# Attention with two gated layers on one core: narrow reciprocals of the softmax sums, and a copy that repeats them

## The chip, the cores and the metric

One core of a Trainium2 chip runs the whole program in one launch. The metric is the time of one execution on the device in microseconds. The engines are PE (matmuls), DVE, ACT, POOL, and SP, which issues the DMAs; each works through its own queue of instructions in order and waits there on semaphores.

## The reference

Causal attention with a decay bias, then a layer with cos as its gate, then an RMS norm and a layer with SiLU as its gate. Four sequences of 576 tokens, 8 heads of 64, 512 columns, all in fp32:

```python
scores = scale * q @ k.T + minimum(-(cum_i - cum_j), 0)     # masked above the diagonal
attn = exp(scores - max) ; attn = attn / (sum(attn) + 1e-9)
x = attn @ v                        # 2304 tokens x 512
h = x @ w_in ; y = (h * cos(h)) @ w_out
xn = y / rms(y) * rms_g
out = (silu(xn @ w_gate) * (xn @ w_val)) @ w_out2
```

## The kernel before

Heads are worked on in 16 pairs (two heads side by side in the 128 partitions). Each pair has two parts: "a" with the first 256 queries and "b" with the other 320; part a is one unit of work, part b is two. For a unit PE forms the scores (lines 433 and 438, and 460 and 461 for the last 64 queries of both heads, called p), DVE copies them out of PSUM with their minimum as a by-product (tile mn, lines 445 and 464), ACT takes the exponentials and their sums (e, ep and rs, line 472), PE transposes the exponentials (line 504), a copy brings them to SBUF (tile P), and PE multiplies them by v (line 549).

The result of line 549 has queries along the free dimension, and must be multiplied by one over the sum of each query. The function norm, called once for a unit, prepares that: POOL scales the sums of two to four columns (line 480, tile rn), DVE takes the reciprocal (line 489) and writes each column 64 times side by side (tile rb, 128x128 for a unit of part b, 128x256 for part a), PE transposes rb in the function av (line 533), so that each query's factor stands in the 64 partitions of its head, a copy brings that to tile xu, and DVE multiplies line 549's result by it. The factors of the p rows go through line 531, which reads rn itself; so line 491 takes the reciprocal of that one column in place.

The two layers are gemms in split form: each fp32 value is a leading part and a residue in a shorter format, and three of the four products are added (lines 651 and 657). The weights are brought into that form in the function chunk: a shift of the exponent on ACT or POOL (line 365 or 364), bit work on POOL and DVE (368, 369, 371), then a copy and a subtraction (288 or 295, and 299 or 301) into tiles wi and ws. These conversions run beside attention, and those of the second layer beside the first layer. Activations (xa, g) are split in the same way.

The order of all instructions is set before the kernel runs by a planner in the same file (class Plan). Each operation names one or more engines with an entered cost, a due time, and the tiles it reads and writes; the planner steps through the engines by these costs and, for an operation with a choice (function copy: ACT, DVE or POOL; function two: DVE or POOL), takes the engine that would be done first. What comes out is one fixed queue for each engine. Line 489 is entered with 128 m + 80 ns, 208 or 336. Gemms have later due times than attention and are put where PE would wait.

Of the kernel before, what the change touches and what calls it, by code (L numbers as in the profile page):

```python
# [195 lines left out]
def dve2(n):  # L196
    return 0.52 * n + 68
# [10 lines left out]
def pool1(n):  # L208
    return 0.833 * n + 161
# [7 lines left out]
def attention_moe_moe(ctx, tc, q2, k2, vp, s, w_in, w_out, w_gate, w_val, w_out2, rms_g, out):  # L217
    nc = tc.nc
    pe, act, dve, pool, sp = nc.tensor, nc.scalar, nc.vector, nc.gpsimd, nc.sync
    plan = Plan()  # L220
# [61 lines left out]
    def on(e, ns, fn):  # L282
        return [(e, ns, fn)]

    def copy(o, i, n, r, w, scale=1.0, psum=False, engines=("ACT", "DVE", "POOL"), **kw):
        alts = []
        if "ACT" in engines:
            alts.append(("ACT", (act_p if psum else act_s)(n), lambda: act.activation(o(), i(), AF.Copy, scale=scale)))  # L288
        if "DVE" in engines:
            if scale == 1.0:  # L290
                alts.append(("DVE", (dve1 if psum else dve2)(n), lambda: dve.tensor_copy(o(), i())))
            else:
                alts.append(("DVE", dve2(n), lambda: dve.tensor_scalar(out=o(), in0=i(), scalar1=scale, scalar2=None, op0=ALU.mult)))
        if "POOL" in engines and not psum:
            alts.append(("POOL", pool1(n), lambda: pool.tensor_scalar(out=o(), in0=i(), scalar1=scale, scalar2=0.0, op0=ALU.mult, op1=ALU.add)))
        return plan.op(alts, r, w, **kw)
# [61 lines left out]
    def chunk(src, w, after=()):  # L358
        raw, g = raw_r.new(), cv_r.new()
        load(raw, lambda: src.bitcast(I32).rearrange("p (c t) -> p c t", t=2), 1 << 19, [], [raw], after=after)  # L360
        top, low = (lambda: raw()[:, :, 1]), (lambda: raw()[:, :, 0])
        v = lambda: g().bitcast(I32)
        plan.op([
            ("POOL", pool1(512), lambda: pool.tensor_scalar(out=g(), in0=top().bitcast(F32), scalar1=2.0 ** -112, scalar2=1.0, op0=ALU.mult, op1=ALU.mult)),
            ("ACT", act_s(512), lambda: act.activation(g(), top().bitcast(F32), AF.Copy, scale=2.0 ** -112)),  # L365
        ], [raw], [g])

        plan.op(on("POOL", pool1(512), lambda: pool.tensor_scalar(out=top().bitcast(F32), in0=top().bitcast(F32), scalar1=0.0, scalar2=1.0, op0=ALU.mult, op1=ALU.mult)), [], [raw])  # L368
        plan.op(on("DVE", dve1(512), lambda: dve.scalar_tensor_tensor(  # L369
            out=top(), in0=low(), scalar=29, in1=top(), op0=ALU.logical_shift_right, op1=ALU.bitwise_or)), [], [raw])  # L370
        plan.op(on("DVE", dve1(512), lambda: dve.scalar_tensor_tensor(  # L371
            out=v(), in0=v(), scalar=3, in1=top(), op0=ALU.logical_shift_left, op1=ALU.bitwise_or)), [raw], [g])
        copy(lambda: w()[:, 0, :], g, 512, [g], [w])
        two(lambda: w()[:, 1, :], g, lambda: w()[:, 0, :].bitcast(F32), 512, [g], [w])
        return w
# [30 lines left out]
    class Part:  # L406
# [69 lines left out]
        def norm(self, keys):  # L476

            rn, rs, a = self.rn, self.rs, self.col[keys[0]]
            b = a + len(keys)
            plan.op(on("POOL", 204, lambda: pool.tensor_scalar(  # L480
                out=rn()[:, a:b], in0=rs()[:, a:b], scalar1=1e-9, scalar2=float(2.0 * np.pi), op0=ALU.add, op1=ALU.mult)), [(rs, self.col[k]) for k in keys], [(rn, a)])
            rb, p = self.rb, "p" in keys
            if self.c == "a":
                o, i = (lambda: rb()), (lambda: rn()[:, :4].rearrange("p (e t) -> p t e", e=2))
            else:
                t = 0 if p else 1
                o, i = (lambda: rb()[:, t:t + 1]), (lambda: rn()[:, a:a + 2].unsqueeze(1))
            m = 1 if self.c == "b" else 2
            plan.op(on("DVE", 128 * m + 80, lambda: dve.reciprocal(out=o(), in_=i().unsqueeze(3).to_broadcast([128, m, 2, 64]))), [(rn, a)], [(rb, a)])  # L489
            if p:  # L490
                plan.op(on("DVE", 150, lambda: dve.reciprocal(out=rn()[:, 2:3], in_=rn()[:, 2:3])), [], [(rn, a)])

        def tr(self, e, i):
            tr = self.bank("T")
# [104 lines left out]
    for b in (s_b, cum):  # L599
# [4 lines left out]
        out=cum()[:, :S], data0=ones.to_broadcast([128, S]), data1=s_b()[:, :S], initial=0.0, op0=ALU.mult, op1=ALU.add)), [(s_b, 0)], [(cum, 0)])  # L604
# [6 lines left out]
    for i, (t, mid) in enumerate(((0, 63), (1, 191), (2, 319), ("p", 543), (3, 447))):  # L611
        o, w = DS[t]
# [9 lines left out]
            out=to(), in0=src(), scalar=halves[:, 1:2], in1=to().bitcast(F32), op0=ALU.mult, op1=ALU.add)), [raw], [(ds, o)], **kw)  # L622
# [126 lines left out]
    for k in range(8 * NB1):  # L749
        j, m = divmod(k, 8)  # L750
# [75 lines left out]
    for n, (d, f, w) in enumerate(names):  # L826
        plan.now = tick_at(8 * NB1)
        b = chunk(w[f], ws_r.new(), [ticks[W3_FROM + n * (W3_TO - W3_FROM) // len(names)]])
# [5 lines left out]
    for n, (d, f, w) in enumerate(names[:len(slots)]):  # L834
# [4 lines left out]
        b = w3[d, f] = slots[n][1].new(slots[n][2])  # L839
# [4 lines left out]
    for n in range(NB2 * F2):  # L844
# [25 lines left out]
        if f == F2 - 1:  # L870
            plan.now = unit_at(n)
            for t in range(3):
                o = u_r.new()
# [59 lines left out]
```

## Time and profile before

| | |
|---|---|
| three runs | 1106.91, 1107.06 and 5998.42 us, median 1107.06 |
| the profiled execution | 1107.06 us, its span 1105.3 us |
| instructions in the span | 17231 |
| DMA | 134.86 MB, 122 GB/s on average |

Times below are microseconds from the start of the span. The profile's page gives busy time by engine and the chain of work that ended last; the trace gives the same by stretch, by line and by tile. Matmuls are pipelined and their ends are modelled: a PE that is shown as busy need not be at its peak, and PEld is the weight load that overlaps it. Line 299 is the helper two on DVE, 301 the same on POOL; 288, 291 and 295 are the helper copy on ACT, DVE and POOL.

### The profile page before, as it was taken

How to read it: one execution, taken by the hardware profiler on the slowest of the kernel's cores; microseconds unless marked ns; L12 is line 12 of the kernel's file. 1: busy time of each engine (PE TensorE's matmuls, PEld its weight loads, DVE VectorE, ACT ScalarE, POOL GpSimd, SP SyncE). 2: the span in 40 equal slices, each digit the busy share in tenths (PEclk: the TensorE clock that was granted, in tenths of full speed). 3: DMA queues.
4: the chain of work that ended last, by engine and by line, in shares of the span. 5: the costliest groups of instructions: out<-in, count | busy, mean ns of one | idle time of the engine just before them, and what ended most of it. 6: DMA issues, size and time to landing. Idle time of an engine off the chain costs nothing.

```text
span 1105.3 us, 17231 instructions
## 1 busy us (share of the span) xinstructions
PE 1084.6 (98%) x6602; PEld 943.7 (85%) x6602; DVE 556.8 (50%) x1182; ACT 515.2 (47%) x1072; POOL 141.7 (13%) x213
## 2 busy tenths in 40 slices
PE   7989999999999999999999999999999999999998
PEld 5667776777788999988999999999999999999997
DVE  8888989675534677778677431121221211211211
ACT  5778889777743565656565332121211211211211
POOL 4631444111000012102010000000000000000000
PEclk9999999999999999999999999999999999999999
DMA  5763775534292364645564951010100100100000
GB/s 198 267 210 127 234 239 186 177 113 139 75 349 76 117 219 172 198 172 176 188 211 130 383 195 48 1 58 1 33 25 1 58 1 1 44 1 1 29 1 29
DMA packets 60595, 134.86 MB, mean 122 GB/s; under 512 B 8544, under 2 KB 28512, under 8 KB 60512
## 3 DMA queue, kind: packets, MB, share of 16 engines
q1 hardware_dynamic: 60512, 133.75, 35.7%
q8 instruction: 52, 0.85, 0.3%
q14 instruction: 31, 0.25, 0.1%
HBM read 94.40 MB, written 39.32 MB: 121 GB/s over the span
## 4 chain that ended last, share of the span: by engine, by line
PE 83%; DVE 9%; ACT 3%; issue 3%; POOL 1%; DMA 1%; DVEq 0%; POOLq 0%; ACTq 0%
PE bank L651 43%; PE bank L657 29%; PE bank L549 3%; PE bank L504 3%; PE bank L433 2%; DVE cv L371 2%; DVE e L445 1%; DVE rb L489 1%; DVE raw L369 1%; DVE u L299 1%; PE bank L741 1%; DVE ws L299 1%; PE bank L460 1%; ACT P L288 1%; ACT e L472 0%
## 5 line engine op out<-in xcount | busy, mean ns | idle before, releaser
L299 DVE TENSOR_TENSOR u<-bank,u 128x512 f32<-128x512 f32 (+1 forms) x144 | 89.8, 623 | 338.7 <-PE bank L651 269.2
L657 PE MATMUL bank<-wr,g 128*128 128x512 f32 x942 | 234.0, 396 | 0.6 <-ACT g L288 0.5
L651 PE MATMUL bank<-xa,wi 128*128 128x256 f32 x1728 | 220.8, 283 | 0.0
L651 PEld LDWEIGHTS bank<-xa,wi 128*128 128x128 f32 x1728 | 215.0, 188 | 6.0 <-issue 0.6
L288 ACT ACTIVATE g<-u 128x512 fp32r<-128x512 f32 (+1 forms) x132 | 76.1, 577 | 280.1 <-DVE u L299 280.0
L657 PEld LDWEIGHTS bank<-wr,g 128*128 128x128 f32 x942 | 173.1, 188 | 35.6 <-ACT g L288 1.2
L299 DVE TENSOR_TENSOR g<-u,g 128x384 fp32r<-128x384 f32 (+1 forms) x130 | 81.2, 625 | 63.4 <-ACT g L288 61.9
L651 PE MATMUL bank<-xb,wi 128*128 128x384 f32 x528 | 102.9, 339 | 0.0
L651 PE MATMUL bank<-xb,wr 128*128 128x384 f32 x528 | 101.0, 335 | 0.0
L651 PEld LDWEIGHTS bank<-xb,wi 128*128 128x128 f32 x528 | 93.3, 188 | 3.0 <-DVE xb L299 1.7
L651 PEld LDWEIGHTS bank<-xb,wr 128*128 128x128 f32 x528 | 93.1, 188 | 2.1
L767 ACT ACTIVATE u<-bank,quarter 128x512 int32<-128x512 f32 x72 | 49.2, 684 | 71.1 <-PE bank L651 70.4
L472 ACT ACTIVATE e<-e,mn 128x128 f32<-128x128 f32 (+3 forms) x128 | 70.8, 555 | 18.1 <-DVE mn L445 17.6
L657 PE MATMUL bank<-ws,g 128*128 128x512 f32 x300 | 77.7, 399 | 1.3 <-ACT g L288 1.3
L299 DVE TENSOR_TENSOR u<-u,bank 128x512 f32<-128x512 int32 x72 | 49.1, 682 | 57.9 <-ACT u L767 57.1
L368 POOL TENSOR_SCALAR raw<-raw 128x512 f32<-128x512 f32 x68 | 47.2, 694 | 234.6 <-ACT cv L365 227.5
L769 ACT ACTIVATE u<-u,half_pi 128x512 f32<-128x512 f32 x72 | 52.2, 725 | 45.9 <-DVE u L299 45.6
L860 ACT ACTIVATE u<-bank 128x384 f32<-128x384 f32 x72 | 35.4, 492 | 71.2 <-PE bank L651 60.8
L657 PE MATMUL bank<-wi,g 128*128 128x512 f32 x270 | 65.9, 391 | 0.0
L288 ACT ACTIVATE P<-bank 128x384 f32<-128x384 f32 (+3 forms) x135 | 52.9, 425 | 26.4 <-PE bank L504 25.5
L657 PEld LDWEIGHTS bank<-ws,g 128*128 128x128 f32 x300 | 54.0, 188 | 12.9 <-ACT g L288 1.6
L489 DVE RECIPROCAL rb<-rn 128x128 f32<-128x128 f32 (+1 forms) x48 | 58.1, 1213 | 13.3 <-POOL rn L480 12.7
(127 smaller groups left out, 1400.7 us busy)
## 6 DMA issues: line engine op xcount, KB each, us to landing
w_d<-ws SPq DMA_DIRECT2D x32, 512.0 KB, 2.9
raw<-in_w_out_dram SPq DMA_DIRECT2D x28, 512.0 KB, 4.8
raw<-in_w_in_dram SPq DMA_DIRECT2D x16, 512.0 KB, 4.2
wo_d<-ws SPq DMA_DIRECT2D x16, 512.0 KB, 3.4
ws<-wo_d SPq DMA_DIRECT2D x16, 512.0 KB, 3.6
wr<-wo_d SPq DMA_DIRECT2D x16, 512.0 KB, 6.0
wi<-w_d SPq DMA_DIRECT2D x16, 512.0 KB, 5.1
wr<-w_d SPq DMA_DIRECT2D x16, 512.0 KB, 5.2
```

Of the source, the lines that this page charges most:

```text
L288: alts.append(("ACT", (act_p if psum else act_s)(n), lambda: act.activation(o(), i(), AF.Copy, scale=scale)))
L299: alts = on("DVE", dve1(n), lambda: dve.tensor_tensor(out=o(), in0=a(), in1=b(), op=op))
L368: plan.op(on("POOL", pool1(512), lambda: pool.tensor_scalar(out=top().bitcast(F32), in0=top().bitcast(F32), scalar1=0.0, scalar2=1.0, op0= ...
L472: plan.op(on("ACT", act_s(w) + 187, lambda E=E, o=o, w=w, i=i: act.activation(E()[:, o:o + w], E()[:, o:o + w], AF.Exp, scale=-1.0, bias=s ...
L489: plan.op(on("DVE", 128 * m + 80, lambda: dve.reciprocal(out=o(), in_=i().unsqueeze(3).to_broadcast([128, m, 2, 64]))), [(rn, a)], [(rb, a)])
L504: pe.transpose(tr()[:m, 128 * j:128 * j + 128], E[0]()[:, E[2] + c:E[2] + c + m], ident)
L549: pe.matmul(X()[64 * e:64 * e + 64, lo:hi], vr()[:kk, e, c, :], p[e], start=(c == 0), stop=(c == jobs[-1][0]))
L651: pe.matmul(h, w[:, a, 128 * k:128 * k + 128], x[k // 2][:, k % 2, c, :blk], start=(n == 0), stop=(n == 11))
L657: pe.matmul(acc[t], g[a][:, 128 * t:128 * t + 128], w[:, c, :], start=(first and (a, c) == (0, 0)), stop=(last and (a, c) == (1, 0)))
L767: plan.op(on("ACT", act_p(512) + 93, lambda u=u, h=h: act.activation(u().bitcast(I32), h(), AF.Identity, bias=quarter)), [h], [u])
L769: plan.op(on("ACT", act_s(512) + 93, lambda u=u: act.activation(u(), u(), AF.Sin, scale=-TWO_PI, bias=half_pi)), [], [u], table="sin")
L860: plan.op(on("ACT", act_p(BLK2), lambda us=us, h=hs[0]: act.activation(us(), h()[:, :BLK2], AF.Silu)), [hs[0]], [u], table="silu")
```

## The change

The reciprocal is taken in place of the narrow columns rn (2, 3 or 4 of them, with the p column among the three), always on DVE and entered with 204 ns. Then the helper copy repeats each column 64 times into rb, on ACT, DVE or POOL as the planner finds. The separate reciprocal of the p column goes, since the three-column one holds it.

```diff
--- before.py
+++ after.py
@@ -479,16 +479,15 @@
             b = a + len(keys)
             plan.op(on("POOL", 204, lambda: pool.tensor_scalar(
                 out=rn()[:, a:b], in0=rs()[:, a:b], scalar1=1e-9, scalar2=float(2.0 * np.pi), op0=ALU.add, op1=ALU.mult)), [(rs, self.col[k]) for k in keys], [(rn, a)])
-            rb, p = self.rb, "p" in keys
+            plan.op(on("DVE", 204, lambda: dve.reciprocal(out=rn()[:, a:b], in_=rn()[:, a:b])), [], [(rn, a)])
+
+            rb = self.rb
             if self.c == "a":
-                o, i = (lambda: rb()), (lambda: rn()[:, :4].rearrange("p (e t) -> p t e", e=2))
+                o, i, m = (lambda: rb()), (lambda: rn()[:, :4].rearrange("p (e t) -> p t e", e=2)), 2
             else:
-                t = 0 if p else 1
-                o, i = (lambda: rb()[:, t:t + 1]), (lambda: rn()[:, a:a + 2].unsqueeze(1))
-            m = 1 if self.c == "b" else 2
-            plan.op(on("DVE", 128 * m + 80, lambda: dve.reciprocal(out=o(), in_=i().unsqueeze(3).to_broadcast([128, m, 2, 64]))), [(rn, a)], [(rb, a)])
-            if p:
-                plan.op(on("DVE", 150, lambda: dve.reciprocal(out=rn()[:, 2:3], in_=rn()[:, 2:3])), [], [(rn, a)])
+                t = 0 if "p" in keys else 1
+                o, i, m = (lambda: rb()[:, t:t + 1]), (lambda: rn()[:, a:a + 2].unsqueeze(1)), 1
+            copy(o, lambda: i().unsqueeze(3).to_broadcast([128, m, 2, 64]), 128 * m, [(rn, a)], [(rb, a)])
 
         def tr(self, e, i):
             tr = self.bank("T")
```

Entered costs have changed, so the planner's queues change too. The names in the pieces of order: rn and rs are the scaled and the plain sums, rb the repeated ones, numbers are buffers; raw, cv, ws, wi are a weight's conversion, e and ep exponentials, bank a PSUM bank. From line 492 on the changed kernel's lines are one lower.

On DVE, the end of the second pair's three-column group. Before:

```order
L371 SCALAR_TENSOR_TENSOR cv_132<-cv_132,raw_131 128x512
L299 TENSOR_TENSOR xu_177<-bank_154,xu_177 128x320
L489 RECIPROCAL rb_190<-rn_188 128x128
L491 RECIPROCAL rn_188<-rn_188 128x1
L445 ISA e_173,mn_184<-bank_156,cm_166 128x512
```

And changed, at the same place:

```order
L371 SCALAR_TENSOR_TENSOR cv_132<-cv_132,raw_131 128x512
L371 SCALAR_TENSOR_TENSOR cv_133<-cv_133,raw_130 128x512
L482 RECIPROCAL rn_188<-rn_188 128x3
L299 TENSOR_TENSOR ws_125<-cv_133,ws_125 128x512
L299 TENSOR_TENSOR xu_177<-bank_154,xu_177 128x320
L445 ISA e_173,mn_184<-bank_156,cm_166 128x512
```

The two reciprocals have become one of three columns, one weight conversion (cv_133, ws_125) has come forward around it, and the scores e_173 follow the multiplication into xu_177 directly.

On ACT, behind the exponentials of the second pair's last unit, before:

```order
L288 ACTIVATE P_181<-bank_153 128x3x128
L288 ACTIVATE P_182<-bank_154 128x3x128
L288 ACTIVATE P_181<-bank_153 128x64
L365 ACTIVATE cv_132<-raw_130 128x512
L288 ACTIVATE P_182<-bank_154 128x64
L288 ACTIVATE ws_126<-cv_133 128x512
```

And changed:

```order
L288 ACTIVATE P_181<-bank_153 128x3x128
L288 ACTIVATE P_182<-bank_154 128x3x128
L288 ACTIVATE P_181<-bank_153 128x64
L288 ACTIVATE rb_190<-rn_188 128x128
L288 ACTIVATE P_182<-bank_154 128x64
L365 ACTIVATE cv_132<-raw_130 128x512
```

The spreading copy rb_190 stands between two evictions of P, and the second weight conversion (ws_126) has left ACT at this place.

Counted over the whole order, the 48 spreading copies are 27 of 128 columns and 11 of 256 on ACT, 5 and 1 on DVE, and 4 of 256 on POOL. ACT's table loads are 29 in both. PE has the same number of instructions in both.

## Rows read from the trace of the kernel before

**Rows 1.** Page, part 1: busy us of each engine (share of the span) xinstructions.
```profile
PE 1084.6 (98%) x6602; PEld 943.7 (85%) x6602; DVE 556.8 (50%) x1182; ACT 515.2 (47%) x1072; POOL 141.7 (13%) x213
```

**Rows 2.** Page, part 4, the chain by engine; then the chain by line.
```profile
PE 83%; DVE 9%; ACT 3%; issue 3%; POOL 1%; DMA 1%; DVEq 0%; POOLq 0%; ACTq 0%
...
by line: PE bank L651 43.2%; PE bank L657 28.8%; PE bank L549 3.2%; issue 2.9%; PE bank L504 2.9%; PE bank L433 2.0%; DVE cv L371 1.6%; DVE e L445 1.4%; DVE rb L489 1.1%; DVE raw L369 1.0%; DVE u L299 0.8%; PE bank L741 0.7%; DVE ws L299 0.
```

**Rows 3.** Windows: us; busy us of PE, PEld, DVE, ACT, POOL; PEclk; DMA; GB/s.
```profile
20.00:80.00 60.00, 53.53 (x386) 34.83 (x383) 53.44 (x137) 45.13 (x130) 27.11 (x39) 1.00 0.68 222
80.00:200.00 120.00, 116.02 (x832) 86.58 (x832) 106.05 (x245) 102.08 (x236) 44.13 (x65) 1.00 0.58 194
200.00:300.00 100.00, 99.86 (x715) 75.90 (x714) 62.39 (x173) 74.21 (x180) 11.48 (x26) 1.00 0.42 130
300.00:1105.00 805.00, 799.80 (x4593) 734.51 (x4591) 316.98 (x568) 284.70 (x505) 50.33 (x61) 1.00 0.29 100
```

**Rows 4.** Source, line 549: duration ns min/median/max, first and last start us, forms.
```profile
L549 PE MATMUL bank<-P,vr x448: 219/404/484, 17.2 to 305.6; 128*64 128x320 f32 x62, 128*64 128x192 f32 x23, 128*64 128x256 f32 x22, 128*64 128x64 f32 x22
```

**Rows 5.** Windows, matmuls of line 549 alone (P by v).
```profile
20.00:80.00 60.00, 12.85 (x112) 7.54 (x112) 1.00 0.68 222
80.00:200.00 120.00, 19.44 (x168) 11.31 (x168) 1.00 0.58 194
200.00:300.00 100.00, 16.39 (x140) 10.46 (x140) 1.00 0.42 130
```

**Rows 6.** Windows, line 651 alone (first gemm).
```profile
80.00:200.00 120.00, 25.96 (x190) 23.25 (x189) 1.00 0.58 194
200.00:300.00 100.00, 19.54 (x144) 17.78 (x144) 1.00 0.42 130
```

**Rows 7.** Windows, line 657 alone (second gemm).
```profile
80.00:200.00 120.00, 19.20 (x72) 12.73 (x72) 1.00 0.58 194
200.00:300.00 100.00, 19.39 (x72) 12.68 (x72) 1.00 0.42 130
```

**Rows 8.** Chain in order of time, 360 to 372: start us, us, what.
```profile
364.83 2.84 PE bank L651 x24
367.67 2.79 PE bank L657 x12
```

**Rows 9.** Chain by line: 80 to 200 us, then 200 to 300 us.
```profile
by line: issue 12.1%; PE bank L549 8.0%; PE bank L651 6.9%; DVE cv L371 6.8%; DVE raw L369 5.6%; DVE e L445 5.6%; DVE rb L489 5.1%; DVE ws L299 4.9%; PE bank L504 4.2%; PE bank L433 3.9%; ACT cv L365 2.5%; ACT P L288 2.4%; DVE u L299 2.3%; 
...
by line: PE bank L504 19.2%; PE bank L651 16.1%; PE bank L657 15.8%; PE bank L549 15.7%; PE bank L433 13.8%; PE bank L460 3.8%; PE bank L438 3.3%; PE bank L533 2.9%; issue 2.8%; DVE e L445 2.1%; PE bank L531 1.3%; PE bank L741 1.1%; PE bank
```

**Rows 10.** Timeline, 54 to 59: start us, us, what [idle before <-releaser].
```profile
55.06 1.74 DVE L489 RECIPROCAL rb<-rn 128x256 f32<-128x256 f32 x1
...
58.47 0.78 ACT L472 ACTIVATE ep<-ep,mn 128x576 f32<-128x576 f32 x1 [1.21 <-DVE mn L464]
```

**Rows 11.** Groups by form, reciprocals: busy us, mean ns | idle before.
```profile
L489 DVE RECIPROCAL rb<-rn 128x128 f32<-128x128 f32 x32 | 30.3, 946 | 9.6 <-POOL rn L480 9.1
L489 DVE RECIPROCAL rb<-rn 128x256 f32<-128x256 f32 x16 | 28.0, 1748 | 3.8 <-POOL rn L480 3.6
...
L491 DVE RECIPROCAL rn<-rn 128x1 f32<-128x1 f32 x16 | 1.9, 121 | 0.0
```

**Rows 12.** Groups by form, the copies nearest to the new ones.
```profile
L288 ACT ACTIVATE xu<-bank 128x256 f32<-128x256 f32 x15 | 5.6, 375 | 0.0
...
L288 ACT ACTIVATE P<-bank 128x64 f32<-128x64 f32 x27 | 5.4, 227 | 0.6 <-DVE P L291 0.4
...
L295 POOL TENSOR_SCALAR pk<-pick 128x128 fp32r<-128x128 f32 x13 | 5.2, 397 | 27.1 <-PE bank L461 26.9
...
L291 DVE CAST pk<-pick 128x128 fp32r<-128x128 f32 x3 | 0.7, 248 | 0.0
```

**Rows 13.** Page, part 5: subtractions of residues on DVE.
```profile
L299 DVE TENSOR_TENSOR g<-u,g 128x384 fp32r<-128x384 f32 (+1 forms) x130 | 81.2, 625 | 63.4 <-ACT g L288 61.9
```

**Rows 14.** Waits: engine line waited for: us in total, times, longest us.
```profile
DVE rb L489 <- POOL rn L480: 12.7, 10, 2.6
```

## The prediction

> **What bounds the kernel now.** I read the page's busy times first [rows 1]: PE is busy for 98% of the span, DVE for 50%, ACT for 47%. That average hides two stages, so next comes the chain that ended last [rows 2]: 83% of it is PE and 9% DVE, and one group of DVE stands in it by name, the reciprocals of line 489, with 1.1% of 1105.3 us, that is 12.2 us. The table by stretches [rows 3] shows where. From 300 us to the end PE is busy for 799.8 of 805 us and DVE for 317: there only the gemms of lines 651 and 657 run, and nothing that DVE saves can matter. From 20 to 80 us and from 80 to 200 us DVE is busy for 53.4 of 60 (89%) and 106.1 of 120 us (88%); from 200 to 300 us for 62.4 of 100. The reciprocals all lie before 300 us, so the forecast is about the first 300 us, in which attention runs, from 80 us on with gemms between its pieces.
>
> A busy PE is not PE at its peak, so I ask what one pair of heads costs. Line 549 makes 448 matmuls, 28 for each of the 16 pairs, the last at 305.6 us [rows 4]. In 20 to 80 us there are 112 [rows 5], 4.0 pairs with no gemm to speak of: 15.0 us a pair. In 80 to 200 us there are 168, 6.0 pairs, and beside them 190 matmuls of line 651 and 72 of line 657 [rows 6, 7]. In a dense stretch 24 of line 651 take 2.84 us and 12 of line 657 take 2.79 us [rows 8], 0.118 and 0.2325 us each; so the gemms take 22.5 + 16.7 = 39.2 us and leave 80.8 us, 13.5 us a pair. In 200 to 300 us it is 140, 5.0 pairs, with 144 and 72 gemm matmuls, 33.7 us: 66.3 us are left, 13.3 us a pair. The same attention work holds PE for 15.0 us where DVE is 89% full and PE has nothing to put into its waits, for 13.5 us where gemms fill them, and for 13.3 us where DVE is 62% full. In the chain of 200 to 300 us [rows 9] nearly all lines are PE's; in 80 to 200 us DVE's lines and "issue" fill much of it.
>
> The timeline at 55 us shows the mechanism [rows 10]: a reciprocal of 128x256 holds DVE for 1.74 us; behind it stand two weight conversions and the second half of the ep scores, and ACT idles 1.21 us for their minimum (mn) before it can start the exponentials.
>
> **The change part by part.** It removes 32 reciprocals of 128 columns (30.3 us), 16 of 256 (28.0 us) and 16 of one column (1.9 us) [rows 11]: 60.2 us of DVE. It adds 48 narrow ones, 16 each of 2, 3 and 4 columns. From 128 to 256 columns the time grows by 1748 - 946 = 802 ns, 6.27 ns a column, and one column takes 121 ns; so 2, 3 and 4 columns come to about 127, 134 and 140 ns, and 16 of each to 6.4 us. The trace shows no width between 1 and 128; the bounds are 121 ns (5.8 us in all) and a straight line through the two wide ones, 946 - 126 x 6.27 = 156 ns (7.5 us).
>
> Against this split speaks a rule of the Trainium skill, "VectorE: DVE Perf Modes", section on the TRN2 errata: Vector and Scalar instructions that read SBUF pay a fixed cost each, so that many small tiles pay it many times, and tiles of at least 512 elements are advised. The one-column row agrees that there is such a floor (121 ns, where the skill's 58 cycles and one element at 0.96 GHz would be 61 ns). By the same section's figure for ScalarE (224 cycles plus one per element, 1.2 GHz) the 38 copies on ACT would take about 12.3 us, an estimate. So the rule holds here as far as the floor goes, and the sum below has paid it 96 times.
>
> The spreading copies go where the planner sends them: 27 of 128 columns and 11 of 256 to ACT, 5 and 1 to DVE, 4 of 256 to POOL, counted in the order. No row has this copy on ACT; the nearest copies take 227 ns for 64 columns and 375 ns for 256 [rows 12], 0.77 ns a column, hence 276 ns for 128: 27 x 0.276 + 11 x 0.375 = 11.6 us on ACT. On DVE a copy of a repeated column, 128 wide, takes 248 ns, on POOL 397 ns [rows 12]; 5 x 0.25 + 0.4 = 1.7 us on DVE. Four times 0.4 to 0.8 us on POOL, busy for 83 of 280 us [rows 3], stay beside its other work. With new costs the planner also shifts work of others: DVE gets four more residue subtractions net (g, wi and xa come, ws go), 4 x 0.625 = 2.5 us [rows 13], and three more small copies, about 1 us. So DVE loses 60.2 - 6.4 - 1.7 - 3.5 = 48.6 us, 3.04 us a pair. ACT loses some weight conversions to POOL, which I leave as margin. PE's order stays: the gemms stand between the same attention pieces within a few positions, and the first gemm comes between the ninth and the tenth part in both.
>
> What is late next? With 3.04 us gone from each of the 4 and 6 pairs of the two early stretches, DVE comes to 53.4 - 12.2 = 41.2 of 60 and 106.1 - 18.2 = 87.9 of 120 us. ACT stands at 45.1 and 102.1 [rows 3] and gets 0.72 us more a pair, so 48 of 60 and 106 of 120: from then on ACT and PE are the fuller ones, and the time cannot shrink by what DVE saves. I therefore take the third stretch as the model, where DVE is light already.
> - 20 to 80 us: 4.0 pairs from 15.0 to 13.3 us, 6.8 us.
> - 80 to 200 us: 6.0 pairs from 13.5 to 13.3 us, 1.2 us.
> - Before 20 us only part of a pair's reciprocals lie, and loads and the preparation of the bias hold the start too; I take a third of one pair's saving, 1.0 us (bounds 0 and 3).
> - The 13.3 us themselves: the chain of 200 to 300 us still has DVE's scores with 2.1% and "issue" with 2.8% [rows 9], 4.9 us or 0.98 us a pair. Bounds 0 and 0.98; since only part of this waits for reciprocals I take 0.36 us for 15 pairs, 5.4 us.
>
> Sum 14.4 us. The profiled execution took 1107.06 us around its span of 1105.3 us, and 1107.06 us is the median of the runs too: 1107.1 - 14.4 = 1092.7 us, 1.3% less. Behind 300 us nothing changes; the gain is kept because PE has hardly a wait there for the change to touch (5.2 us idle in 805 us [rows 3]). What a measurement of this kernel can tell from no change is taken as 2%, 22 us.
>
> **The rivals.**
> First, DVE is the whole bound until 200 us. For it: DVE is 88 and 89% busy there [rows 3], and the stall of [rows 10]. Then all of its saving there comes off: 10 pairs x 3.04 + 1.0 = 31.4 us, 1075.7 us, 2.8% faster. Against it: ACT would have to do its 106 us of the second stretch in some 102.
>
> Second, the reciprocals are hidden. The first stretch may be paced by hand-overs, by DMA (busy share 0.68 there [rows 3]) and by ACT, and from 80 us PE is 97% busy. Then only the 1.2 us of the second stretch and about 2 us elsewhere go: 1104 us. Against it: 12.2 us of the chain are reciprocals by name, and the stall of [rows 10].
>
> Third, slower: ACT becomes the bound by waiting. A copy on ACT needs POOL's scaling and then DVE's narrow reciprocal, and everything behind it in ACT's queue (exponentials, evictions of P that free PSUM banks) waits with it. From 20 to 300 us ACT is busy for 221.4 of 280 us and gets about 11 us: 47.6 us of room. 38 copies fill it when each holds ACT for 1.25 us; from 1.8 us it costs over 2%. Before, DVE waited for POOL's scaling in 10 of 48 cases, 12.7 us, at most 2.6 us [rows 14]. At 2 us each it would be 76 - 48 = 28 us more, 1135 us. Against it: the order sets the copy behind several other ACT instructions in most places, and a DVE that is less full answers sooner.
>
> **How the numbers follow.** Forecast 0.62, own range 1083 to 1101; DVE the whole bound 0.17; hidden 0.16; slower 0.05. The range from 1076 to 1105 takes in the first two rivals' times and leaves out the third. Faster by over 2% (below 1084.9 us): most of the first rival and a little of the forecast's end, 0.20. Slower by over 2%: 0.04. The rest, 0.76, lies within 2%.
>
> **What would show it.** In the profile after: narrow reciprocals at 0.12 to 0.16 us, DVE at about 508 us in all, the copies on ACT near 0.28 and 0.38 us; line 549's matmuls counted by stretch should give about 13.3 us a pair already before 80 us, and the last of them should start near 291 us instead of 305.6. The forecast is wrong if the pair before 80 us still takes 15 us (hidden), if it falls below 12 us (first rival), or if ACT's idle time in front of the rb copies sums to more than some 48 us (third). A stretch behind the last line 549 other than the 799.7 us of before would mean that the reordering, not the reciprocals, moved the time.

## The result and the profile after

The changed kernel took 1097.28 us (median of four runs, 1096.31 to 1098.46), before 1107.05 us beside it: 0.9913 of the time, 95% interval 0.9893 to 0.9932. That is 9.8 us less, where 14.4 us had been forecast; the interval stops short of 1, and the change is within 2%. The profiled execution took 1096.31 us, 10.75 us less than the one of before. One run of before (5998.42 us) is left out of the ratio, and the four runs of the changed kernel fall into two pairs, 1096.3 and 1096.4 us at a mean granted clock of 0.999 and 1.000, and 1098.2 and 1098.5 us at 0.998; the profiled one is of the first pair.

The page's busy times and its chain by engine, after:

```profile
PE 1081.8 (99%) x6602; PEld 944.4 (86%) x6602; DVE 522.9 (48%) x1179; ACT 519.3 (47%) x1101; POOL 144.3 (13%) x219
...
PE 90%; DVE 5%; issue 2%; POOL 2%; ACT 1%; DMA 0%; POOLq 0%; DVEq 0%; ACTq 0%
```

DVE has lost 33.9 us against [rows 1], not 48.6. The chain [rows 2] is PE's to 90% in place of 83%, DVE's share fell from 9 to 5%, and no reciprocal stands among the lines that its list names any more.

The windows of [rows 3] after (the span now ends at 1094.5 us), and under them line 548 alone (549 before, [rows 5]):

```profile
20.00:80.00 60.00, 58.67 (x425) 41.49 (x424) 47.54 (x143) 50.54 (x153) 30.40 (x46) 1.00 0.71 236
80.00:200.00 120.00, 117.67 (x843) 87.96 (x842) 99.26 (x255) 104.08 (x242) 46.98 (x67) 1.00 0.63 206
200.00:300.00 100.00, 100.00 (x729) 76.42 (x728) 45.68 (x156) 74.93 (x183) 6.74 (x22) 1.00 0.38 118
300.00:1105.00 805.00, 789.08 (x4516) 725.95 (x4514) 313.69 (x563) 279.46 (x497) 50.24 (x61) 1.00 0.29 99
```

```profile
20.00:80.00 60.00, 14.79 (x112) 10.58 (x112) 1.00 0.71 236
80.00:200.00 120.00, 18.88 (x168) 11.01 (x168) 1.00 0.63 206
200.00:300.00 100.00, 18.29 (x160) 10.87 (x160) 1.00 0.38 118
```

From 80 us on PE's busy share hardly moves; it is DVE's that falls, most from 200 to 300 us. Before 80 us ACT is now the fuller of the two (50.5 us, DVE 47.5). There are again 112 matmuls of v (line 548: P by v) from 20 to 80 us, but gemms have come in behind them, and 160 from 200 to 300 us, the last now at 295.1 us where it was at 305.6 [rows 4]:

```profile
L548 PE MATMUL bank<-P,vr x448: 219/404/484, 16.0 to 295.1; 128*64 128x320 f32 x66, 128*64 128x256 f32 x23, 128*64 128x64 f32 x22, 128*64 128x128 f32 x20
```

Behind it 799.4 us are left, 799.7 before: nearly all of the gain lies in the attention stage, and all of it is kept.

A finer reckoning than by windows goes pair by pair. The start of every 28th matmul of v is read from the timeline, and from the distance of two such starts 0.1185 us is taken off for each matmul of the first gemm between them and 0.2325 us for each of the second, the prices of a dense stretch [rows 8]. Means in us a pair, and when the first pair ends:

```
kernel                 pair 1 ends   pairs 2-4   5-10   11-15   last matmul of v
before                     29.7         15.0     13.7    13.0        305.6
changed                    27.1         13.8     13.2    12.7        295.1
e1_same_order              28.1         14.0     12.9    12.8        295.3
e8_no_spread               27.2         13.8     12.8    12.8        293.2
e7_no_bitwork              29.1         14.2     12.7    12.8        295.7
e9_half                    28.4         14.1     13.1    12.8        297.1
e4_no_copy                 28.8         14.0     13.3    13.3        301.8
e10_depth3                 29.9         15.0     13.7    12.6        304.4
e3_twice                   37.9         18.7     16.6    15.4        354.3
```

The other kernels in the table are the experiments below. Its first column is not a fair comparison throughout: from 0 to 20 us the granted clock was 1.00 before, in the changed kernel, e8_no_spread and e10_depth3, 0.91 in e1_same_order, e9_half and e4_no_copy, 0.83 in e7_no_bitwork and 0.95 in e3_twice.

Of the 10.5 us at the last matmul of v, 2.6 lie in the first pair, 3.7 in pairs 2 to 4, 2.7 in pairs 5 to 10 and 1.5 behind.

The new instructions, groups by form as in [rows 11, 12]:

```profile
L288 ACT ACTIVATE rb<-rn 128x128 f32<-128x128 f32 x27 | 8.2, 305 | 5.0 <-DVE rn L482 4.9
...
L288 ACT ACTIVATE rb<-rn 128x256 f32<-128x256 f32 x11 | 4.5, 407 | 1.2 <-DVE rn L482 1.2
...
L482 DVE RECIPROCAL rn<-rn 128x4 f32<-128x4 f32 x16 | 2.8, 175 | 8.2 <-POOL rn L480 8.2
L482 DVE RECIPROCAL rn<-rn 128x3 f32<-128x3 f32 x16 | 2.8, 173 | 7.6 <-POOL rn L480 7.4
L291 DVE COPY rb<-rn 128x128 f32<-128x128 f32 x5 | 2.7, 539 | 0.0
...
L482 DVE RECIPROCAL rn<-rn 128x2 f32<-128x2 f32 x16 | 2.6, 162 | 2.5 <-POOL rn L480 2.1
...
L295 POOL TENSOR_SCALAR rb<-rn 128x256 f32<-128x256 f32 x4 | 2.0, 510 | 2.2 <-PE bank L461 1.1 <-PE bank L460 0.7 <-DVE rn L482 0.4
```

The narrow reciprocal takes 162 to 175 ns, the copies on ACT 305 and 407 ns (12.7 us in all, 11.6 forecast), those of 128 columns on DVE 539 ns. The stall of [rows 10], in the same place of the third pair (timeline, columns as there):

```profile
51.07 0.17 DVE L482 RECIPROCAL rn<-rn 128x4 f32<-128x4 f32 x1
...
52.95 0.51 DVE L464 CUSTOM_DVE_ANT_0 ep<-bank,cp,mn 128x288 f32<-128x288 f32 x1
...
53.56 0.78 ACT L472 ACTIVATE ep<-ep,mn 128x576 f32<-128x576 f32 x1 [0.31 <-DVE mn L464]
```

The four-column reciprocal is 0.17 us where 1.74 us stood, and ACT waits 0.31 us for the minimum of ep in place of 1.21. The waits that belong to the new chain:

```profile
DVE rn L482 <- POOL rn L480: 17.7, 12, 2.6
...
ACT rb L288 <- DVE rn L482: 6.1, 10, 1.3
```

DVE waits for POOL's scaling 17.7 us in all (12.7 before, [rows 14]), ACT for the narrow reciprocal 6.1 us in 10 of 38 cases.

### The profile page after: what moved, and what is told of

Its sections match the earlier page's. It is cut to its first block, busy times and chain, and to the rows that moved or that the text cites. A ratio compares the mean times of both kernels' runs of the same rounds, so it can differ in the third digit from the quotient of the medians.

```text
span 1094.5 us, 17279 instructions
## 1 busy us (share of the span) xinstructions
PE 1081.8 (99%) x6602; PEld 944.4 (86%) x6602; DVE 522.9 (48%) x1179; ACT 519.3 (47%) x1101; POOL 144.3 (13%) x219
## 4 chain that ended last, share of the span: by engine, by line
PE 90%; DVE 5%; issue 2%; POOL 2%; ACT 1%; DMA 0%; POOLq 0%; DVEq 0%; ACTq 0%
PE bank L650 44%; PE bank L656 30%; PE bank L503 5%; PE bank L548 4%; PE bank L433 3%; PE bank L460 1%; DVE cv L371 1%; PE bank L438 1%; PE bank L740 1%; PE bank L532 1%; DVE u L299 1%; POOL raw L368 0%; DVE raw L369 0%; DVE ws L299 0%; DVE e L445 0%
## 5 line engine op out<-in xcount | busy, mean ns | idle before, releaser
L288 ACT ACTIVATE g<-u 128x384 fp32r<-128x384 f32 (+1 forms) x133 | 76.7, 577 | 277.1 <-DVE u L299 277.1
L299 DVE TENSOR_TENSOR g<-u,g 128x512 fp32r<-128x512 f32 (+1 forms) x135 | 85.2, 631 | 64.8 <-ACT g L288 63.3
L445 DVE CUSTOM_DVE_ANT_0 e<-bank,cm 128x128 f32<-128x128 f32 (+3 forms) x128 | 57.2, 485 | 20.8 <-PE bank L438 20.2
```

Of the source, the lines that this page charges most:

```text
L299: alts = on("DVE", dve1(n), lambda: dve.tensor_tensor(out=o(), in0=a(), in1=b(), op=op))
L445: plan.op(on("DVE", dve1(w) + 17, lambda o=o, w=w, i=i, e=e: dve.tensor_tensor_reduce(out=Es[e]()[:, o:o + w], in0=Sp[e]()[:, o:o + w], in ...
```

## The experiments

All were measured beside runs of before (1106.84 to 1107.07 us).

**The same work in the old order.** The planner's queues stay as they were, instruction by instruction; only the wide reciprocal's place on DVE is taken by the narrow one and a copy.

```diff
-            plan.op(on("DVE", 128 * m + 80, lambda: dve.reciprocal(out=o(), in_=i().unsqueeze(3).to_broadcast([128, m, 2, 64]))), [(rn, a)], [(rb, a)])
+            c = b - 1 if p else b
+            def both():
+                dve.reciprocal(out=rn()[:, a:c], in_=rn()[:, a:c])
+                dve.tensor_copy(o(), i().unsqueeze(3).to_broadcast([128, m, 2, 64]))
+            plan.op(on("DVE", 128 * m + 80, both), [], [(rn, a), (rb, a)])
```

> Every queue keeps the order of before; only the wide reciprocal is replaced, in its own place on DVE, by a narrow reciprocal and a copy right behind it (the one-column reciprocal of the p column stays). Theory A, the time comes from what DVE no longer does: DVE loses 60.2 - 1.9 - 48 x 0.17 - 48 x about 0.38 = 32 us, about as much as in the changed kernel, so about 1097 us (1094 to 1100). Theory B, the gain comes from the order that the planner made of the new costs: 1104 to 1108 us. Theory C, the copies on ACT held the changed kernel back: below 1094 us.

Measured: 1096.31 us, ratio 0.9904 (0.9887 to 0.9920). Page, part 1:

```profile
PE 1081.9 (99%) x6602; PEld 942.3 (86%) x6602; DVE 527.2 (48%) x1230; ACT 514.4 (47%) x1072; POOL 143.1 (13%) x213
```

DVE has 29.6 us less than before, ACT has none of the copies, POOL none, the order is old, and the gain is the changed kernel's, whose interval overlaps. So the gain needs neither the order that came with the new costs nor the copies on ACT.

**The old work with true costs.** The wide reciprocals stay, and the planner is told what they take.

```diff
-            plan.op(on("DVE", 128 * m + 80, lambda: dve.reciprocal(out=o(), in_=i().unsqueeze(3).to_broadcast([128, m, 2, 64]))), [(rn, a)], [(rb, a)])
+            plan.op(on("DVE", 802 * m + 144, lambda: dve.reciprocal(out=o(), in_=i().unsqueeze(3).to_broadcast([128, m, 2, 64]))), [(rn, a)], [(rb, a)])
```

> The wide reciprocals of before stay; the planner is told what they take (946 and 1746 ns in place of 208 and 336), so that it places them, and moves other work from DVE, with that in view. Theory A: DVE's work stays about the same, 1103 to 1108 us. Theory B, order is what counts: about 1097 us (1092 to 1101).

Measured: 1111.01 us, ratio 1.0039 (1.0025 to 1.0052), 4 us slower and above either range. DVE's total is the same (page, part 1):

```profile
PE 1085.2 (98%) x6602; PEld 943.8 (85%) x6602; DVE 556.6 (50%) x1175; ACT 517.0 (47%) x1073; POOL 150.4 (14%) x219
```

The old work in a new order gave a loss here. That an order from nearer costs would be a better one is not borne out.

**The wide reciprocals twice.**

```diff
-            plan.op(on("DVE", 128 * m + 80, lambda: dve.reciprocal(out=o(), in_=i().unsqueeze(3).to_broadcast([128, m, 2, 64]))), [(rn, a)], [(rb, a)])
+            def twice():
+                for _ in range(2):
+                    dve.reciprocal(out=o(), in_=i().unsqueeze(3).to_broadcast([128, m, 2, 64]))
+            plan.op(on("DVE", 128 * m + 80, twice), [(rn, a)], [(rb, a)])
```

> Before with every wide reciprocal done twice, same order. Theory A: DVE gets 58 us more, 3.65 us a pair. Before 80 us a pair takes 13.3 + 3.65 = 17 us of DVE and, at 89% full, 19 us; from 80 to 200 us 17.7 + 3.65 = 21.3 us where a pair had 20; so 4 x 4 + 6 x 2.5 = 31 us more and a little behind it: 1130 to 1150 us. Theory B, or the reciprocals hidden: within 10 us of before.

Measured: 1154.51 us, ratio 1.0430 (1.0415 to 1.0446): 47.7 us more, at the upper edge and beyond. Part 1 of its page, then its windows in the columns of [rows 3]:

```profile
PE 1103.8 (96%) x6602; PEld 956.1 (83%) x6602; DVE 612.7 (53%) x1230; ACT 516.9 (45%) x1072; POOL 142.0 (12%) x213
```

```profile
20.00:80.00 60.00, 47.65 (x295) 29.93 (x292) 53.02 (x117) 35.37 (x102) 23.71 (x33) 0.87 0.53 164
80.00:200.00 120.00, 105.14 (x718) 78.18 (x714) 107.48 (x227) 87.92 (x202) 36.21 (x54) 0.96 0.52 174
200.00:300.00 100.00, 92.14 (x610) 68.78 (x611) 83.35 (x187) 70.28 (x168) 20.13 (x36) 0.95 0.42 137
```

DVE has 55.9 us more and is busy for 88 to 90% until 200 us; nearly all of it shows in the time. The last column but two is the granted clock: 0.87 from 20 to 80 us and 0.96 and 0.95 behind, where before had 1.00. PE was busy for 47.7 of those first 60 us (53.5 before), and where its clock was lowered its own work took longer: a matmul of v of 320 columns 741 ns in place of 432 (medians of 35 and 152). So a part of the 47.7 us is the clock's and not DVE's alone; how much was not measured.

**A part of the dose.** As in the first experiment, but only part a's 256-column reciprocals are replaced.

```diff
-            plan.op(on("DVE", 128 * m + 80, lambda: dve.reciprocal(out=o(), in_=i().unsqueeze(3).to_broadcast([128, m, 2, 64]))), [(rn, a)], [(rb, a)])
+            def both():
+                if self.c == "b":
+                    dve.reciprocal(out=o(), in_=i().unsqueeze(3).to_broadcast([128, m, 2, 64]))
+                else:
+                    dve.reciprocal(out=rn()[:, a:b], in_=rn()[:, a:b])
+                    dve.tensor_copy(o(), i().unsqueeze(3).to_broadcast([128, m, 2, 64]))
+            plan.op(on("DVE", 128 * m + 80, both), [], [(rn, a), (rb, a)])
```

> As e1_same_order, but only the sixteen 256-column reciprocals of part a become a narrow one and a copy; those of part b stay wide. DVE loses 28.0 - 16 x (0.175 + 0.35) = 19.6 us, two thirds of the 29.6 us of e1_same_order. If each us of DVE is worth the same until it is spent: 1100 us. If DVE's relief runs out gradually (the doubled reciprocals cost 0.82 us a us, the first ones removed are worth more than the last): 1097 to 1099 us. If the gain belongs to part b's chain: above 1102 us.

Measured: 1098.67 us, ratio 0.9927 (0.9910 to 0.9943). Page, part 1:

```profile
PE 1082.8 (99%) x6602; PEld 942.4 (86%) x6602; DVE 538.3 (49%) x1198; ACT 514.2 (47%) x1072; POOL 141.7 (13%) x213
```

18.5 us of DVE bought 8.2 us. All of them are part a's, so this run does not tell apart that the first us pay more from that part a's reciprocals do.

**No spreading at all.** Order of before, DVE does the narrow reciprocals alone. The transposes read a constant rb (set to ones once, which the diff leaves out), so every row but p is left without its factor.

```diff
+            c = b - 1 if p else b
+            plan.op(on("DVE", 128 * m + 80, lambda: dve.reciprocal(out=rn()[:, a:c], in_=rn()[:, a:c])), [], [(rn, a), (rb, a)])
```

> The order of before, as in e1_same_order, but DVE does only the narrow reciprocals; the spreading is left out (PE transposes a tile rb that is set once to ones, so that the factors of all rows but p are missing). DVE loses some 18 us more than in e1_same_order. If DVE were still a bound of the early pairs, at e1's rate of 10.5 us for about 32 us of DVE, this is 6 us faster than e1_same_order: about 1090 us, and pairs 2 to 4 fall from 14.0 us towards 13. If DVE's relief is spent (PE and ACT hold the rest): 1094 to 1097 us, pairs 2 to 4 at 13.5 us or more.

Measured: 1095.83 us, ratio 0.9900 (0.9883 to 0.9918). Page, part 1:

```profile
PE 1081.5 (99%) x6602; PEld 944.0 (86%) x6602; DVE 513.4 (47%) x1182; ACT 513.9 (47%) x1072; POOL 144.2 (13%) x215
```

DVE has another 13.8 us less than in e1_same_order (the copies were shorter there than the 18 us expected), and the time is 0.5 us less, with overlapping intervals. In one row, DVE's total and the median: 612.7 us and 1154.5; 556.8 and 1106.9; 538.3 and 1098.7; 527.2 and 1096.3; 513.4 and 1095.8. A us of DVE is worth 0.85, 0.44, 0.21 and 0.04 us in turn; the first holds the lowered clock of e3_twice, the second stands for part a's reciprocals, and the intervals of the last three medians overlap from one to the next. The changed kernel stands where the curve has gone flat.

**What holds the first pairs then?** First, the weights' conversions beside them: the exponent shift and the bit work are left out for the first layer, on top of the edit of e1_same_order (not shown again).

```diff
+        if not after:
+            f = lambda: raw()[:, :, 1].bitcast(F32)
+            copy(lambda: w()[:, 0, :], f, 512, [raw], [w])
+            two(lambda: w()[:, 1, :], f, lambda: w()[:, 0, :].bitcast(F32), 512, [raw], [w])
+            return w
```

> e1_same_order without the exponent shift and the bit work on the first layer's weights (lines 365 or 364, 368, 369, 371 for w_in and w_out; the copy and the residue stay and read the upper words): the layer's weights are wrong. The planner's order changes with it, so only the first pairs are compared, where no gemm runs. If the weights' conversions in ACT's, DVE's and POOL's queues hold pairs 2 to 4: 12.3 to 13.0 us a pair in place of 14.0. If the hand-overs inside the pair hold them: 13.5 us or more.

Measured once: 1097.14 us; pairs 2 to 4 took 14.2 us each. The window from 20 to 80 us, columns as in [rows 3]:

```profile
20.00:80.00 60.00, 57.95 (x423) 40.16 (x421) 34.85 (x129) 45.01 (x133) 12.83 (x24) 1.00 0.67 220
```

DVE is down to 34.9 of 60 us and POOL to 12.8, and the pairs are no faster. So, as far as one run in another order of the planner can show it, the time of the shift and the bit work does not hold them. Then the depth of the pipeline, again on top of e1_same_order:

```diff
-DEPTH = 2
+DEPTH = 3
```

> e1_same_order with three units open in place of two (DEPTH): transposes and the product with v stand one unit later on PE, so each hand-over from scores over exponentials to transposes has a unit more time; the planner's order changes. If hand-overs hold pairs 2 to 4 at 14.0 us: 12.5 to 13.2 us a pair, and 1092 to 1095 us in all. If PE's own work holds them, or the buffers of e (two each) do: 13.5 us or more and 1096 us or slower.

Measured: 1104.11 us, ratio 0.9975 (0.9966 to 0.9985), pairs 2 to 4 at 15.0 us: slower than e1_same_order by 7.8 us. More time for the hand-overs with the same buffers, in the order that the planner makes of it, does not help; a new order can cost some us by itself (e2_true_cost), and the granted clock was 0.97 from 20 to 80 us here. What keeps pairs 2 to 4 at 13.8 to 14.2 us, where later ones reach 12.6 to 12.8, stays open between hand-overs, buffers and PE's order there.

**The copies' own price.** Without them, PE reads each narrow reciprocal as a repeated column (the diff leaves out that the copy and tile rb go):

```diff
-                    pe.transpose(R()[:, 128 * t:128 * t + 128], rb()[:, t].rearrange("p e m -> p (e m)"), ident)
+                    for e in range(2):
+                        i = self.col[e, t + (2 if self.c == "b" else 0)]
+                        pe.matmul(R()[64 * e:64 * e + 64, 128 * t:128 * t + 128], rn()[:, i:i + 1].to_broadcast([128, 64]), ident, start=True, stop=True)
```

> The changed kernel without the spreading copies and without tile rb: PE reads the narrow reciprocals themselves as repeated columns against the identity (as line 531 does for the p column), four matmuls of 64 columns in place of two transposes a part. ACT loses 12.7 us, DVE 3 us, one hand-over goes. Theory C (copies or their hand-over cost): 1088 to 1094 us. Theory A with ACT not the bound: 1094 to 1098 us. If the 64-column matmuls cost PE 0.1 us more each, 64 x 0.1 = 6 us come back.

Measured: 1102.60 us, ratio 0.9961 (0.9946 to 0.9976), 5.3 us slower than the changed kernel. Its page's part 1, a part's factors in its chain (start us, us, what), and then the same factors in the changed kernel's chain:

```profile
PE 1090.9 (99%) x6794; PEld 950.2 (86%) x6794; DVE 513.9 (47%) x1168; ACT 515.6 (47%) x1071; POOL 141.4 (13%) x212
```

```profile
211.35 0.59 PE bank L526 x8
```

```profile
207.91 0.22 PE bank L532 x2
```

The 128 matmuls of this kind leave 256 records, the 64 transposes left 64, and a part's factors take 0.59 us in place of 0.22. PE's total rises by 9.1 us, and pairs 11 to 15 take 13.3 us each, 12.7 in the changed kernel, whose PE is busy for all of the 100 us from 200 to 300: there PE has no room. Pairs 5 to 10 are hardly longer on average (13.3 and 13.2). The last sentence of the expectation had the mechanism and about the size.

**All copies on ACT.**

```diff
-            copy(o, lambda: i().unsqueeze(3).to_broadcast([128, m, 2, 64]), 128 * m, [(rn, a)], [(rb, a)])
+            copy(o, lambda: i().unsqueeze(3).to_broadcast([128, m, 2, 64]), 128 * m, [(rn, a)], [(rb, a)], engines=("ACT",))
```

> The changed kernel with all 48 spreading copies on ACT (10 more there, 10 x 0.33 = 3.3 us, none on DVE or POOL). If waits on ACT were the price that kept the gain below the forecast, each moved copy costs a hand-over of about 1 us: over 1100 us. If ACT has room: 1094 to 1099 us.

Measured: 1096.81 us, ratio 0.9907 (0.9890 to 0.9925), the changed kernel's time. ACT has the room, and its waits were not the price. No version tried is faster than the changed kernel by more than the measurement can tell.

## Why the prediction came out as it did

Sign, size class and place were right; the gain was forecast at 14.4 us and is 9.8 (10.75 in the profiled execution, 10.5 of it up to the last matmul of v).

DVE as the holder of the early pairs: shown. The same order with DVE relieved gives the whole gain (e1_same_order), the opposite dose 47.7 us (e3_twice). What PE waits for agrees with it. Two lines of the waits before, then two after (columns as in [rows 14]):

```profile
PE bank L460 <- DVE mn L445: 2.5, 3, 1.1
PE bank L504 <- DVE mn L445: 2.1, 4, 1.3
```

```profile
PE bank L548 <- DVE mn L445: 0.9, 2, 0.5
PE bank L503 <- DVE mn L445: 0.8, 2, 0.4
```

Added over all lines, PE's matmuls wait for DVE's minimum (mn) 8.7 us before, 2.3 after, 1.7 in e1_same_order and 29.7 in e3_twice. For the factors rn and rb themselves the matmuls wait in no line of the view, and the weight loads for 1.6 us before. By these waits the wide reciprocals cost time because the scores stood behind them on DVE, not because their own results came late.

The terms of the sum, one by one:

- What DVE loses: 48.6 us forecast, 33.9 measured. The narrow reciprocals took 8.2 us, not 6.4; the line through the two wide forms (156 ns), named as a bound, was nearer than the one-column row. DVE's copies took 3.0 us, not 1.7, and the bit work of lines 369 and 371, unchanged in number, 5.0 us more. The other 6.6 us are spread over many lines and are not explained here. This error cost little, since e8_no_spread shows the next 13.8 us to be worth 0.5.
- The four terms together put every pair at 13.3 - 0.36 = 12.94 us, and so they are compared with the table pair by pair. By the end of pair 4, at 74.7 us before, they give 1.0 us and 3.65 pairs of 15.0 - 12.94 = 2.06 us, 8.5 us; the table has 6.3. Pairs 5 to 10 should give 6 x 0.56 = 3.4 us and give 2.7, pairs 11 to 15 should give 5 x 0.36 = 1.8 us and give 1.5. The last 0.7 of the 14.4 us are the rest of the stretch up to 80 us.
- Before 20 us, 1.0 us: about right; the first matmul of v starts 1.2 us earlier (16.0 us, 17.2 before).
- Pairs of 20 to 80 us at 13.3 us and less: this is where the sum failed, with 2 to 3 of the 3.9 us that are missing (14.4 forecast, 10.5 in the table). Pairs 2 to 4 fell from 15.0 to 13.8 only. The later stretch, with gemms between the pieces of attention, was taken as the model of one without, and there a light DVE does not bring that level: 14.2 us at 58% DVE in e7_no_bitwork. Little of the difference is recorded as idle time of PE, which is busy for 58.7 of 60 us after; the matmuls of v last longer instead, 14.79 us for 112 of them against 18.29 us for 160 behind 200 us, which is 3.7 and 3.2 us a pair. Why, no run shows.
- 80 to 200 us: the changed kernel does not reach 12.94 us there either (13.2 us a pair), but e1_same_order and e8_no_spread do (12.9 and 12.8), so from the fifth pair on the level itself was sound.
- The 0.36 us: in the changed kernel pairs 11 to 15 alone come below 12.94 us, with 12.7. Little was left to gain there, since PE was busy for 99.86 of 100 us before already [rows 3], and e4_no_copy shows that more work of PE goes into the time: 0.37 us more a part comes out as 0.6 us a pair. The chain of 200 to 300 us after has no line of DVE among those listed:

```profile
by line: PE bank L503 19.5%; PE bank L650 19.0%; PE bank L548 17.5%; PE bank L656 17.3%; PE bank L433 12.1%; PE bank L460 4.8%; PE bank L532 3.3%; PE bank L438 2.8%; PE bank L530 1.6%; PE bank L461 1.3%; PE bank L740 0.9%
```

- The first rival, DVE as the whole bound, would have been 1075.7 us: the time stops following DVE long before. The second, hidden, 1104: refuted by e1_same_order. The third, ACT's waits: copies on ACT wait 6.1 us in all where 48 us would have been needed, and e5_act_only is no slower.

## What to carry to other kernels

An engine that is 89% busy in a stage can be worth relieving, but not without end: 63% of the relief (18.5 of 29.6 us of DVE, part a's) brought 78% of the gain here (8.2 of 10.5 us), and the last 13.8 us nothing that could be told from none. A full engine shows in what the bound engine waits for: here not the result of the slow operation, but the work queued behind it. Before pricing a gain by a later, lighter stretch, ask what else differs there; and to tell an operation's price from the planner's new order, put the new operation into the old one's place in the queue.

## What the runs showed of the hardware that was not expected

Copies on DVE had two speeds. In e1_same_order, the tile view of rb (duration ns min/median/max, first and last start us):

```profile
L493 DVE COPY rb<-rn x48: 226/294/1226, 14.3 to 287.8; 128x128 f32<-128x128 f32 x32, 128x256 f32<-128x256 f32 x16
```

Of the 32 copies of 128 columns 21 took 226 to 229 ns, of the 16 of 256 columns 13 took 293 to 295 ns. The other 14 took 351 to 1226 ns. Each of these began while a POOL instruction was running, and ended 78 to 84 ns after that one had (128 columns) or 146 to 150 ns (256). The longest, in the timeline:

```profile
38.89 1.27 POOL L301 TENSOR_TENSOR wi<-cv,wi 128x512 fp32r<-128x512 f32 x1
...
39.08 1.23 DVE L493 COPY rb<-rn 128x256 f32<-128x256 f32 x1
```

POOL's subtraction ends at 40.16 us, the copy at 40.31. A copy in front of a POOL instruction, or one whose POOL neighbour ended within its first 135 ns, kept the short time (six cases). This agrees with the Trainium skill, "GPSIMD Engine Reference", section "Key points", which says that POOL shares its SBUF interfaces with VectorE and that they contend when a DVE instruction runs in a two-port mode or has two SBUF inputs. In which mode these copies ran no trace shows; that the wait lasts to the end of the POOL instruction is read from these runs. The changed kernel shows it again: four of its five DVE copies of 128 columns began while POOL was running, took 0.31 to 1.08 us and ended about 0.08 us behind POOL, and the fifth took 0.23 us.

The second is the clock in e3_twice: with DVE the bound and PE busy for 47.7 of 60 us, PE's granted clock was 0.87 from 20 to 80 us, a mix of its levels of 1.2 and 2.4 GHz, where the kernel before had 1.00 with PE busy for 53.5. By the matmul of v of 320 columns, 741 ns at the lower level and 432 at the higher, such a stretch costs PE time beyond the wait itself.
